# Second stage's input product by a seven-product block algorithm over pairs of token tiles, that stage ordered by the list scheduler

## The chip, the cores and the metric

One core of a Trainium2 chip runs the whole program in one launch. The metric is the device time of that launch in microseconds (us), the median of three runs. TensorE (PE) multiplies, VectorE (DVE), ScalarE (ACT) and GpSimd (POOL) work on vectors, and SyncE (SP) starts the DMA transfers. Each engine works off its own queue in program order and waits on semaphores for the others.

## The reference

Attention over 4 x 8 heads with 576 tokens (a banded mask for half of the heads, a dilated one for the others), whose output is the 2304 x 512 input of a gated layer, whose output is the input of a second layer:

```
def _moe2_ref(x, w_in, w_out, g_ln):          # 2304 tokens, 512 -> 1024 -> 512, float32
    h = x @ w_in
    h_max = np.max(h, axis=-1, keepdims=True)
    e = np.exp(h - h_max)
    sm = e / (np.sum(e, axis=-1, keepdims=True) + 1e-09)
    solu = h * sm
    mu = np.mean(solu, axis=-1, keepdims=True)
    var = np.mean((solu - mu) ** 2, axis=-1, keepdims=True)
    ln = (solu - mu) / np.sqrt(var + 1e-06) * g_ln
    return (ln @ w_out).astype(np.float32)
```

This second layer is the second stage; the change is about its first product, `h = x @ w_in`.

## The kernel before

**Products.** Every float32 operand is split into a high half (rounded to a short form) and a low half (the rest), and a product is three matmuls: high by high, high by low, low by high. One matmul takes 128 rows of the sum (k), 128 tokens and 512 columns. With the tokens' 128 x 128 block as the stationary operand, a tile of 128 tokens needs 2 column halves x 4 k blocks x 3 = 24 matmuls for `h` (`p_h`, L990 to L992) and 8 x 3 = 24 for the output (`p_products`, L1029 to L1031).

**First stage.** Attention and gated layer are ordered by a planner, the class `Plan`. A step has engines with estimated costs, needs, buffers that it takes and uses, and a due number. A simulated clock picks the steps one by one, and the order so found is the order of the instructions on every engine. The last steps of the first stage are the products `y` of the last 512 tokens; each of the four `y` banks is copied out (`yo`), stored to DRAM (`yT`), and read again by the second stage.

**Second stage.** It stands after the planned part, in an order written out by hand: `p_h(0)`, `p_h(1)`, then for each tile i `p_t(i)`, `p_h(i + 2)` and `p_o(i)`. After `p_h` come, for a 128 x 1024 tile, the maximum over the two banks of `h` (DVE L995), the exponential (ACT L997), three small operations and the product by `h` (DVE L1000), the square (ACT L1004), the subtraction of the mean (DVE L1005); then `p_t` turns the tile by 8 transposes on PE (L1015), with high halves by ACT (L1018) and low halves by DVE (L1019). `p_load` reads one tile of tokens back with one DMA (L974), and `p_split` makes its halves (L980, L981).

**Weights.** `prepare(2, ...)` turns the 16 blocks of `w_in` and `w_out` from 64 bit floats into split halves, in planned steps beside the last part of the first stage: per block a shift (ACT), `parts` and `joined` (DVE), `halves` (ACT), `lows` (POOL or DVE).

Of the kernel before, what the change touches and what calls it, by code (L numbers as in the profile page):

```python
# [240 lines left out]
def tile_attention_glu_solu(ctx: ExitStack, tc: tile.TileContext, qk_d, v_d, w1_d, win2_d, wout2_d,  # L241
# [14 lines left out]
    ps = pg.enter_context(tc.tile_pool(name="ps", bufs=1, space=PSUM, side="right"))
# [18 lines left out]
                 "yl": 3, "yh": 3, "pw": 2})  # L275
# [35 lines left out]
    def prepare(stage, f, cuts, srcs, scales, dues, needs=()):  # L311
# [658 lines left out]
    def p_load(i):  # L970
        y = pool["yp"].tile([P, KD, P], F32, tag="y", name="y", bufs=3)
        p = max(x for x in range(len(PARTS)) if start[x] <= i * P)
        a = i * P - start[p]
        nc.sync.dma_start(out=y, in_=yT[p][:, :, a:a + P])  # L974
        y2[i] = y

    def p_split(i):
        y = y2[i]
        yh = pool["yp"].tile([P, 2, KD, P], F32R, tag="yh", name="yh", bufs=3)
        nc.scalar.copy(yh[:, 0], y)  # L980
        nc.vector.tensor_tensor(yh[:, 1], y, yh[:, 0], ALU.subtract)  # L981
        y2[i] = yh

    def p_h(i):
        yh = y2.pop(i)
        h = pool["psh"].tile([P, 2, 512], F32, tag="h", name="h")
        for n in range(2):
            for k in range(KD):
                w = w2[divmod(2 * k + n, 3)]
                nc.tensor.matmul(h[:, n], yh[:, 0, k], w[:, 0], start=(k == 0), stop=False)  # L990
                nc.tensor.matmul(h[:, n], yh[:, 0, k], w[:, 1], start=False, stop=False)  # L991
                nc.tensor.matmul(h[:, n], yh[:, 1, k], w[:, 0], start=False, stop=(k == KD - 1))  # L992
        hf = h.rearrange("p a b -> p (a b)")
        st = pool["sp2"].tile([P, 8], F32, tag="st", name="st", bufs=3)
        nc.vector.tensor_reduce(st[:, 0:1], hf, AX.X, ALU.max, negate=True)  # L995
        e = pool["hp"].tile([P, FF2], F32, tag="e", name="e")
        nc.scalar.activation(e, hf, AF.Exp, bias=st[:, 0:1], accum_out=st[:, 1:2])  # L997
# [10 lines left out]
        ln_t[i] = (e, st)

    def p_t(i):  # L1010
        e, st = ln_t[i]
        tp = pool["pst"].tile([P, NF2, P], F32, tag="t", name="tp", bufs=1)
        lt = pool["hp"].tile([P, 2, NF2, P], F32R, tag="lt", name="lt")
        for k in range(NF2):
            nc.tensor.transpose(tp[:, k, :], e[:, k * P:(k + 1) * P], ident)  # L1015
        for q in range(2):
            c = slice(q * NF2 // 2, (q + 1) * NF2 // 2)
            nc.scalar.copy(lt[:, 0, c], tp[:, c])  # L1018
            nc.vector.tensor_tensor(lt[:, 1, c], tp[:, c], lt[:, 0, c], ALU.subtract)  # L1019
        ln_t[i] = (lt, st)  # L1020

    def p_products(i, ks, a=0, n=DM):
        lt, st = ln_t[i][0:2]
        if ks[0] == 0:
            ln_t[i] = (lt, st, pool["pst"].tile([P, n], F32, tag="o", name="o"))
        o = ln_t[i][2]
        for k in ks:
            w = w2[divmod(8 + k, 3)][:, :, a:a + n]
# [4 lines left out]

# [178 lines left out]
```

## Time and profile before

| | |
|---|---|
| device time, median of 3 runs | 758.14 us (757.66 to 759.91) |
| span of the profiled execution, first to last instruction | 756.9 us |
| PE busy | 744.9 us, 98% of the span |
| DVE, ACT, POOL busy | 399.8, 310.2, 105.3 us |
| second stage's first matmul | 538.02 us after the start |

A span is what the trace shows between the first and the last instruction. The profiled execution's own device time is not listed apart from it: the listed times lie 0.8 to 3.0 us above this span, the median 1.24 us. An engine is busy while an instruction runs on it; matmuls overlap in the pipeline, so the distance from start to start tells what one costs, not its duration.

### The profile page before, as it was taken

The page shows a single profiled execution, that of the slowest core. Times are in us where ns is not written, and L with a number is a line of the kernel's source. Part 1 is how long each engine was busy: PE and PEld are TensorE (multiplying, and loading weights), DVE is VectorE, ACT ScalarE, POOL GpSimd, SP SyncE. Part 2 cuts the span into 40 slices and gives each one's busy share as a digit, 9 for nine tenths or more (in the row PEclk, how much of TensorE's full clock was granted, in tenths as well). Part 3 has the DMA queues.
Part 4 walks back from the last instruction along what each step waited for, and adds up shares of the span by engine and source line. Part 5 has one row for each costly group of instructions (what it writes and reads, how often), then busy time and mean ns, then how long its engine had stood idle before and what let it go on. Part 6 is the DMA issues. An engine that isn't in the chain of part 4 may idle for free.

```text
span 756.9 us, 11671 instructions
## 1 busy us (share of the span) xinstructions
PE 744.9 (98%) x4691; PEld 622.8 (82%) x4691; DVE 399.8 (53%) x761; ACT 310.2 (41%) x718; POOL 105.3 (14%) x129
## 2 busy tenths in 40 slices
PE   8899999999999999999999999999999999999997
PEld 6788888899988887888888888888878888888886
DVE  3879996455444344444444437872354544445541
ACT  2876645355233243233334225541243343443433
POOL 0320322222300121201121200000020110101100
PEclk9999999999999999999999999999999999999999
DMA  9996103143021111041111045500201111111101
GB/s 330 405 402 260 33 4 114 64 149 110 16 87 39 61 49 51 0 155 53 71 70 51 1 153 202 187 1 1 69 20 38 56 45 40 55 29 57 49 22 42
DMA packets 34102, 68.90 MB, mean 91 GB/s; under 512 B 3200, under 2 KB 13440, under 8 KB 34048
## 3 DMA queue, kind: packets, MB, share of 16 engines
q1 hardware_dynamic: 34048, 68.16, 25.6%
q8 instruction: 37, 0.61, 0.3%
q14 instruction: 17, 0.14, 0.1%
HBM read 58.71 MB, written 9.44 MB: 90 GB/s over the span
## 4 chain that ended last, share of the span: by engine, by line
PE 93%; DMA 2%; DVE 2%; ACT 1%; SPq 1%; issue 0%; POOL 0%; ACTq 0%; DVEq 0%; POOLq 0%
PE y L850 7%; PE g L850 7%; PE vp L850 7%; PE g L851 7%; PE g L852 7%; PE y L852 7%; PE y L851 7%; PE vp L852 6%; PE vp L851 6%; PE o L1031 4%; PE h L992 4%; PE h L990 4%; PE h L991 4%; PE o L1029 4%; PE o L1030 4%; DMA raw<-w 2%
## 5 line engine op out<-in xcount | busy, mean ns | idle before, releaser
L850 PE MATMUL y<-uh,w 128*128 128x512 f32 (+1 forms) x244 | 91.6, 376 | 0.0
L852 PE MATMUL y<-uh,w 128*128 128x512 f32 (+1 forms) x244 | 89.2, 366 | 0.0
L851 PE MATMUL y<-uh,w 128*128 128x512 f32 (+1 forms) x244 | 89.1, 365 | 0.0
L881 ACT ACTIVATE u<-g 128x512 f32<-128x512 f32 (+1 forms) x61 | 33.5, 549 | 127.6 <-PE g L852 127.6
L887 DVE SCALAR_TENSOR_TENSOR u<-u,g 128x512 f32<-128x512 f32 (+1 forms) x61 | 38.1, 625 | 88.6 <-ACT u L881 88.4
L850 PE MATMUL vp<-xh,w 128*128 128x512 f32 (+1 forms) x196 | 77.9, 397 | 0.0
L850 PE MATMUL g<-xh,w 128*128 128x512 f32 (+1 forms) x196 | 77.6, 396 | 0.0
L852 PE MATMUL g<-xh,w 128*128 128x512 f32 (+1 forms) x196 | 76.1, 388 | 0.0
L851 PE MATMUL g<-xl,w 128*128 128x512 f32 (+1 forms) x196 | 76.0, 388 | 0.0
L852 PE MATMUL vp<-xh,w 128*128 128x512 f32 (+1 forms) x196 | 75.7, 386 | 0.0
L851 PE MATMUL vp<-xl,w 128*128 128x512 f32 (+1 forms) x196 | 75.5, 385 | 0.0
L891 DVE SCALAR_TENSOR_TENSOR u<-u,vp 128x512 f32<-128x512 f32 (+1 forms) x61 | 38.2, 626 | 53.2 <-PE vp L852 52.8
L286 ACT CAST uh<-u 128x512 fp32r<-128x512 f32 (+1 forms) x61 | 34.8, 571 | 75.0 <-DVE u L891 74.7
L1031 PE MATMUL o<-w,lt 128*128 128x512 f32 (+1 forms) x152 | 57.8, 380 | 0.2 <-DVE lt L1019 0.2
L1029 PE MATMUL o<-w,lt 128*128 128x512 f32 (+1 forms) x152 | 57.7, 380 | 0.0
L1030 PE MATMUL o<-w,lt 128*128 128x512 f32 (+1 forms) x152 | 57.5, 378 | 0.0
L990 PE MATMUL h<-w,yh 128*128 128x512 f32 x144 | 57.4, 399 | 0.0
L991 PE MATMUL h<-w,yh 128*128 128x512 f32 x144 | 56.1, 390 | 0.0
L992 PE MATMUL h<-w,yh 128*128 128x512 f32 x144 | 56.1, 390 | 0.0
L1006 POOL TENSOR_SCALAR st<-st 128x1 f32<-128x1 f32 x18 | 13.4, 745 | 287.3 <-ACT sq L1004 166.8
L850 PEld LDWEIGHTS y<-uh,w 128*128 128x128 f32 x244 | 46.0, 188 | 8.1
L852 PEld LDWEIGHTS y<-uh,w 128*128 128x128 f32 x244 | 46.0, 188 | 7.5
(127 smaller groups left out, 1490.5 us busy)
## 6 DMA issues: line engine op xcount, KB each, us to landing
raw<-w SPq DMA_DIRECT2D x36, 512.0 KB, 10.2
vt<-v SPq DMA_DIRECT2D x30, 256.0 KB, 2.7
qk<-qk SPq DMA_DIRECT2D x14, 400.0 KB, 3.7
y<-yT SPq DMA_DIRECT2D x18, 256.0 KB, 3.1
yT<-yo SPq DMA_DIRECT2D x16, 256.0 KB, 2.6
raw<-win SPq DMA_DIRECT2D x8, 512.0 KB, 5.8
raw<-wout SPq DMA_DIRECT2D x8, 512.0 KB, 4.1
out<-ob SPq DMA_DIRECT2D x16, 256.0 KB, 2.1
```

The lines of the kernel that those rows point to most:

```text
L286: nc.scalar.copy(dst, src) if scale is None else nc.scalar.mul(dst, src, scale)
L850: nc.tensor.matmul(acc, wh, xh, start=first, stop=False)
L851: nc.tensor.matmul(acc, wh, xl, start=False, stop=False)
L852: nc.tensor.matmul(acc, wl, xh, start=False, stop=last)
L887: return lambda e: nc.vector.scalar_tensor_tensor(out=u_of(f), in0=u_of(f), scalar=1.0, in1=T["g", v, f], op0=ALU.add, op1=ALU.mult)
L891: return lambda e: nc.vector.scalar_tensor_tensor(out=u_of(f), in0=u_of(f), scalar=0.5, in1=T["vp", v, f], op0=ALU.mult, op1=ALU.mult)
L990: nc.tensor.matmul(h[:, n], yh[:, 0, k], w[:, 0], start=(k == 0), stop=False)
L991: nc.tensor.matmul(h[:, n], yh[:, 0, k], w[:, 1], start=False, stop=False)
L992: nc.tensor.matmul(h[:, n], yh[:, 1, k], w[:, 0], start=False, stop=(k == KD - 1))
L1029: nc.tensor.matmul(o, lt[:, 0, k], w[:, 0], start=(k == 0), stop=False)
L1030: nc.tensor.matmul(o, lt[:, 0, k], w[:, 1], start=False, stop=False)
L1031: nc.tensor.matmul(o, lt[:, 1, k], w[:, 0], start=False, stop=(k == NF2 - 1))
```

## The change

The tokens are taken in nine pairs r of two tiles. A pair's input is a 2 x 2 block matrix of blocks of 128 tokens x 256 k (`a11`, `a12`, `a21`, `a22`), and `w_in` one of blocks of 256 k x 512 columns (`b11` to `b22`). The pair's `h` is then built from seven block products instead of eight, by Winograd's form of Strassen's algorithm:

- sums of the tokens (`p_sums`, four additions of 128 x 256): s1 = a21 + a22, s2 = s1 - a11, s3 = a11 - a21, s4 = a12 - s2
- sums of the weights, once: t1 = b12 - b11, t3 = b22 - b12, t2 = b22 - t1, t4 = b21 - t2
- p1 = a11 b11, p2 = a12 b21, p3 = s4 b22, p4 = a22 t4, p5 = s1 t1, p6 = s2 t2, p7 = s3 t3, each 2 k blocks x 3 = 6 matmuls into one PSUM bank
- p6 and p7 go on top of p1 in its bank `ha`, and p3 on top of p5 in `hb`; p2 is in `hc`, p4 in `hd`. Between them `ha` is copied out three times: s1 (= p1), u2 (= p1 + p6), u3 (= p1 + p6 + p7)
- four block sums, each with its maximum, in one DVE instruction: c11 = p1 + p2, c22 = u3 + p5, c21 = u3 + p4, c12 = u2 + p5 + p3

The exponential and what follows read `h` from SBUF now. The whole stage is planned steps; `line` fixes the order on PE, the planner that on the other engines. A pair is loaded with three DMAs into one of two buffers: pairs with even r into memory free since the attention ended, pairs with odd r into memory of the first stage, which opens at the step `switch`, after the last product of that stage. `w_in`'s blocks and sums are prepared by `operands`, seven blocks for each of the two k blocks.

```diff
-                 "yl": 3, "yh": 3, "pw": 2})
+                 "pw": 2, "ys0": 1, "ys1": 1, "yh0": 1, "yh1": 1,
+                 "hw0": 1, "hw1": 1, "ew0": 1, "ew1": 1, "lt": 2})
...
+        lead = (("in", 0), "joined", "b11")
+        due = 5000 + 30 * j
...
+        def split(x, needs):
+            plan.add((key, "halves", x), {"a": 0.63}, halves(x), needs + needs_of(home[x][0]), uses=[wf], due=due + 5)
+            plan.add((key, "lows", x), {"p": 1.27, "d": 0.68}, lows(x), [(key, "halves", x)], uses=[wf, st, (st, 1)], due=due + 5)
+
+        for x in ("b11", "b22", "b21"):
+            split(x, [(key, "joined", x)])
+        for x, a, b, free in (("t1", "b12", "b11", ["b11"]), ("t3", "b22", "b12", []), ("t2", "b22", "t1", ["b22"]),
+                              ("t4", "b21", "t2", ["b21"])):
+            before = {"t1": [(key, "joined", "b12")], "t3": [(key, "t1"), (key, "joined", "b22")], "t2": [(key, "t3")],
+                      "t4": [(key, "t2"), (key, "joined", "b21")]}[x]
+            plan.add((key, x), {"p": 1.27, "d": 0.68}, combined(x, a, b), before + [(key, "lows", y) for y in free],
+                     uses=[wf, st, (st, 1)], due=due + 6)
+            split(x, [(key, x)])
...
+    def p_load(r):
+        y = pool["y", r % 2].tile([P, 8, 2, P], F32, tag=f"y{r % 2}", name="y")
+        p = max(x for x in range(len(PARTS)) if start[x] <= r * TP)
+        a = r * TP - start[p]
+        nc.sync.dma_start(out=y[:, 1:3].rearrange("p c k t -> p (c k) t"), in_=yT[p][:, :, a:a + P])
+        for c in range(2):
+            nc.sync.dma_start(out=y[:, 3 * c], in_=yT[p][:, 2 * c:2 * c + 2, a + P:a + TP])
+        y2[r] = y
+
+    def p_sums(r, e):
+        y = y2[r]
+        for out_, a, b, op in ((4, 0, 3, ALU.add), (5, 4, 1, ALU.subtract), (6, 1, 0, ALU.subtract), (7, 2, 5, ALU.subtract)):
+            ENG[e].tensor_tensor(y[:, out_], y[:, a], y[:, b], op)
+
+    SETS = (slice(0, 3), slice(3, 7))
+
+    def p_high(r, h, e):
+        if r not in pairs:
+            pairs[r] = pool["y", r % 2].tile([P, 2, 7, 2, P], F32R, tag=f"yh{r % 2}", name="yh")
+        c = SETS[h]
+        put(e, pairs[r][:, 0, c], y2[r][:, 1 + c.start:1 + c.stop])
+
+    def p_low(r, h, e):
+        c = SETS[h]
+        less(e, pairs[r][:, 1, c], y2[r][:, 1 + c.start:1 + c.stop], pairs[r][:, 0, c])
...
+    def p_product(r, a, b, bank, more):
+        o, yh = p_bank(r, bank), pairs[r]
+        for j in range(2):
+            x = LEFT[a]
+            w = w_in[b, j]
+            first, last_ = j == 0 and not more, j == 1
+            nc.tensor.matmul(o, yh[:, 0, x, j], w[:, 0], start=first, stop=False, skip_group_check=True)
+            nc.tensor.matmul(o, yh[:, 0, x, j], w[:, 1], start=False, stop=False, skip_group_check=True)
+            nc.tensor.matmul(o, yh[:, 1, x, j], w[:, 0], start=False, stop=last_, skip_group_check=True)
+
+    def p_sum(r, row, col, kept, bank, n):
+        if n == 0:
+            rows_of[r, row] = pool["sp2"].tile([P, 10], F32, tag="st", name="st", bufs=8)
+        st = rows_of[r, row]
+        nc.vector.tensor_tensor_reduce(out=p_row(r, ("h", row))[:, col], in0=p_row(r, kept), in1=p_bank(r, bank), scale=1.0,
+                                       scalar=st[:, 8:9] if n else -3.4028234e38, op0=ALU.add, op1=ALU.max,
+                                       accum_out=st[:, 8 + n:9 + n])
...
+    def second_stage(stage_1, last):
...
+        add(("switch",), {"s": 0.0}, switch, stage_1, due=4000)
+
+        def pair_steps(r):
+            due = base + 22 * (r - 2)
+            ys, yh, hw, ew = ((x + str(r % 2), (x, r)) for x in ("ys", "yh", "hw", "ew"))
+            p = max(x for x in range(len(PARTS)) if start[x] <= r * TP)
+            add(("load", r), {"s": 1.6}, lambda e: p_load(r), [("opened",) if r % 2 == 0 else ("switch",)] +
+                [("store", p, k) for k in range(KD)], takes=[ys], due=due - 40)
+            add(("sums", r), {"p": 2.9, "d": 1.4}, lambda e: p_sums(r, e), [("load", r)], uses=[ys[1]], due=due - 20)
+            for h, (a, d) in enumerate(((0.85, 0.95), (1.1, 1.25))):
+                add(("yhigh", r, h), {"a": a}, lambda e, h=h: p_high(r, h, e), [("load", r)] + ([("sums", r), ("yhigh", r, 0)] if h else []),
+                    takes=[yh] if h == 0 else [], uses=[ys[1], yh[1]], due=due - 20)
+                add(("ylow", r, h), {"d": d}, lambda e, h=h: p_low(r, h, e), [("yhigh", r, h)], uses=[ys[1], yh[1]], due=due - 20)
+            banks = {x: ("h" + x, r) for x in "abcd"}
+            tags = dict(a="g", b="vp", c="a", d="a")
+
+            def product(x, a, b, bank, more, before):
+                add((x, r), {"t": 6 * mm}, lambda e: p_product(r, a, b, bank, more), before + [("ylow", r, int(a[0] == "s"))],
+                    takes=[] if more else [(tags[bank], banks[bank])], uses=[yh[1], banks[bank]], due=due)
+
+            def kept(x, after_, tile_, tags_):
+                add((x, r), {"a": 0.6, "d": 0.62}, lambda e: put(e, p_row(r, x), p_bank(r, "a")), [(after_, r)],
+                    takes=tags_, uses=[banks["a"], tile_[1]], due=due - 60)
+
+            def total(x, row, col, kept_, bank, n, before):
+                add((x, r), {"d": 0.75}, lambda e: p_sum(r, row, col, kept_, bank, n), before + [(kept_, r)],
+                    uses=[banks[bank], hw[1], ew[1]], due=due - 50)
+
+            product("p1", "a11", "b11", "a", False, [])
+            kept("s1", "p1", hw, [hw])
+            product("p5", "s1", "t1", "b", False, [])
+            product("p6", "s2", "t2", "a", True, [("s1", r)])
+            kept("u2", "p6", hw, [])
+            product("p2", "a12", "b21", "c", False, [])
+            total("c11", 0, 0, "s1", "c", 0, [("p2", r)])
+            product("p7", "s3", "t3", "a", True, [("u2", r)])
+            kept("u3", "p7", ew, [ew])
+            total("c22", 1, 1, "u3", "b", 0, [("p5", r)])
+            product("p4", "a22", "t4", "d", False, [])
+            total("c21", 1, 0, "u3", "d", 1, [("p4", r), ("c22", r)])
+            product("p3", "s4", "b22", "b", True, [("c22", r)])
+            total("c12", 0, 1, "u2", "b", 1, [("p3", r), ("c11", r)])
+            for row in (1, 0):
+                k = (r, row)
+                ends = [("c21", r)] if row else [("c12", r)]
+                add(("neg", *k), {"d": 0.16}, lambda e, row=row: p_neg(r, row), ends, due=due - 10)
+                add(("exp", *k), {"a": 1.3}, lambda e, row=row: p_exp(r, row), [("neg", *k)], uses=[hw[1], ew[1]], due=due)
+                add(("solu", *k), {"d": 1.85}, lambda e, row=row: p_solu(r, row), [("exp", *k)], uses=[hw[1], ew[1]], due=due)
+                add(("sqr", *k), {"a": 1.35}, lambda e, row=row: p_square(r, row), [("solu", *k), ("switch",)], uses=[ew[1]], due=due)
+                add(("centre", *k), {"d": 0.75}, lambda e, row=row: p_centre(r, row), [("sqr", *k)], uses=[ew[1]], due=due)
+                add(("var", *k), {"p": 1.3}, lambda e, row=row: p_spread(r, row), [("sqr", *k)], due=due)
...
+        line = [("out", last, NF1 - 1, 1)] + h(0, "p1", "p5", "p6", "p2", "p7", "p4") + h(1, "p1") + h(0, "p3") + \
+            h(1, "p2", "p5", "p6", "p7", "p4", "p3") + t(0)
+        for q in range(NP):
+            a, b, r = 2 * q, 2 * q + 1, q + 2
+            line += h(r, "p1", "p5", "p6") + [("o", a, 0, 0)] + t(b) + [("o", a, 0, 1)] + h(r, "p2", "p7", "p4")
+            if q < NP - 1:
+                line += [("o", b, 0, 0)] + h(r, "p3") + t(b + 1) + [("o", b, 0, 1)]
+        line += [("o", NT2 - 1, a, q) for a in (0, DM // 2) for q in range(2)]
+        for x, y in zip(line, line[1:]):
+            plan.steps[y]["needs"].append(x)
+            plan.steps[y]["after"].add(x)
 
```

**On PE, where the second stage begins.** Of before, the transposes of the first tile stand behind 48 matmuls of `h` (here the last two), and 24 more and the first output follow; one row of each group stands here.

```order
L991 MATMUL h_5251<-w2_1_4780,yh_4940 128x512
L992 MATMUL h_5251<-w2_1_4780,yh_4940 128x512
L1015 MATMUL tp_5291<-ident_83,e_5240 128x128 x8
L990 MATMUL h_5308<-w0_0_4626,yh_5005 128x512
...
L1029 MATMUL o_5346<-w2_2_4814,lt_5292 128x512
```

Of the change, the first row of each product is shown, six rows each: yh_4577 are the halves of pair 0, yh_5284 those of pair 1, so these are p1, p5, p6, p2, p7, p4 of pair 0, p1 of pair 1, p3 of pair 0, then p2, p5, p6, p7 of pair 1.

```order
L1110 MATMUL ha_5218<-win_4637,yh_4577 128x512
...
L1110 MATMUL hb_5231<-win_4666,yh_4577 128x512
...
L1110 MATMUL ha_5218<-win_4799,yh_4577 128x512
...
L1110 MATMUL hc_5251<-win_4679,yh_4577 128x512
...
L1110 MATMUL ha_5218<-win_4801,yh_4577 128x512
...
L1110 MATMUL hd_5272<-win_4810,yh_4577 128x512
...
L1110 MATMUL ha_5298<-win_4637,yh_5284 128x512
...
L1110 MATMUL hb_5231<-win_4720,yh_4577 128x512
...
L1110 MATMUL hc_5316<-win_4679,yh_5284 128x512
...
L1110 MATMUL hb_5332<-win_4666,yh_5284 128x512
...
L1110 MATMUL ha_5298<-win_4799,yh_5284 128x512
...
L1110 MATMUL ha_5298<-win_4801,yh_5284 128x512
```

Pair 1's first product, which reads halves of a pair loaded behind `switch`, has moved to the seventh place; behind it, p6 and p7 of pair 1 follow each other with nothing between them, and p3 of pair 1 stands one product behind p7.

**On DVE, at the same place.** Of before, the last two copies of `y`, then the first tile's chain:

```order
L290 COPY yo_5188<-y0_4559 128x512
L290 COPY yo_5194<-y2_4570 128x512
L995 TENSOR_REDUCE st_5238<-h_5213 128x1
L998 TENSOR_SCALAR st_5238<-st_5238 128x1
L999 RECIPROCAL st_5238<-st_5238 128x1
L1000 SCALAR_TENSOR_TENSOR e_5240,st_5238<-e_5240,st_5238,h_5213 128x1024
```

Of the change (the three `ISA` rows of 128x512 are c11, c22, c21 of pair 0; y_5260 is pair 1's input, and the row with x4 its four additions; yh_5284 128x768 are the low halves of its blocks a11, a12, a22):

```order
L290 COPY yo_5240<-y2_4568 128x512
L1118 ISA h_5238,st_5270<-h_5238,hc_5251 128x512
...
L1118 ISA h_5238,st_5281<-e_5279,hb_5231 128x512
...
L1118 ISA h_5238,st_5281<-e_5279,hd_5272,st_5281 128x512
...
L1124 TENSOR_SCALAR st_5281<-st_5281 128x1
L1064 TENSOR_TENSOR y_5260<-y_5260 128x256 x4
L295 TENSOR_TENSOR yh_5284<-y_5260,yh_5284 128x768
L1133 TENSOR_SCALAR st_5281<-st_5281 128x1
L1134 RECIPROCAL st_5281<-st_5281 128x1
L1135 SCALAR_TENSOR_TENSOR e_5279,st_5281<-e_5279,st_5281,h_5238 128x1024
```

Pair 1's additions and low halves stand behind c21 of pair 0, which reads `hd` and so the end of p4.

**On ACT, in a later pair.** lt are the high halves of the turned tiles, ha_5781 the bank of pair 4, e_5716 the rows of pair 3:

```order
L286 CAST lt_5771<-tp_5746 128x512
L286 CAST lt_5771<-tp_5753 128x512
L1128 ACTIVATE e_5716,st_5707<-h_5619,st_5707 128x1024
L1142 ACTIVATE sq_5779,st_5718<-e_5716,st_5718 128x1024
L286 CAST yh_5751<-y_5547 128x1024
L286 COPY h_5805<-ha_5781 128x512
```

The copy s1 (last row) stands behind two high halves, an exponential, a square and the high halves of a later pair. Before, ACT had no copy of `h` at all.

## Rows read from the trace of the kernel before

**Rows 1.** The page of the whole span: its head and part 1.

```profile
span 756.9 us, 11671 instructions
PE 744.9 (98%) x4691; PEld 622.8 (82%) x4691; DVE 399.8 (53%) x761; ACT 310.2 (41%) x718; POOL 105.3 (14%) x129
```

**Rows 2.** Waits of PE: engine, line, releaser: us in total, times, longest.

```profile
PE tp L1015 <- DVE e L1005: 1.1, 1, 1.1
```

**Rows 3.** Timeline of PE, start of the second stage: start, us, instruction [idle before].

```profile
538.02 0.39 PE L990 MATMUL h<-w,yh 128*128 128x512 f32 x1
...
543.24 0.39 PE L992 MATMUL h<-w,yh 128*128 128x512 f32 x1
...
548.67 0.39 PE L992 MATMUL h<-w,yh 128*128 128x512 f32 x1
550.14 1.09 PE L1015 MATMUL tp<-ident,e 128*128 128x128 f32 x8 [1.08 <-DVE e L1005]
```

**Rows 4.** The chain that ended last, in order of time: start, us, what.

```profile
543.66 1.24 DVE st L995
544.92 1.22 ACT e L997 x2
546.55 1.30 DVE e L1000 x2
...
549.34 0.76 DVE e L1005
...
562.42 0.87 PE tp L1015 x8
574.20 0.87 PE tp L1015 x8
```

**Rows 5.** Busy time by stretch: PE, PEld, DVE, ACT, POOL, PEclk, DMA, GB/s.

```profile
600.00:640.00 40.00, 40.00 (x191) 33.37 (x190) 19.29 (x33) 15.61 (x26) 3.87 (x6) 1.00 0.16 49
```

**Rows 6.** Groups of instructions by line and shape, DVE and ACT: busy, mean ns.

```profile
L1019 DVE TENSOR_TENSOR lt<-tp,lt 128x512 fp32r<-128x512 f32 x36 | 24.9, 691 | 20.0 <-ACT lt L1018 20.0
L295 DVE TENSOR_TENSOR uh<-u,uh 128x256 fp32r<-128x256 f32 x14 | 6.0, 427 | 3.1 <-ACT uh L286 3.0
L1000 DVE SCALAR_TENSOR_TENSOR e<-e,st,h 128x1024 f32<-128x1024 f32 x18 | 23.0, 1280 | 0.6
L1000 DVE DVE_READ_ACCUMULATOR e<-e,st,h 128x1 f32 x18 | 1.5, 82 | 0.0
...
L286 ACT COPY yo<-y 128x512 f32<-128x512 f32 x8 | 4.7, 586 | 14.5 <-PE y L852 12.3 <-DMA yT<-yo 2.3
...
L286 ACT CAST w<-wf 128x1536 fp32r<-128x1536 f32 x5 | 7.4, 1485 | 3.8 <-DVE wf L348 3.8
```

**Rows 7.** Timeline of SP, then ACT, at the stage's border; last, DMA issues: us to landing.

```profile
536.90 3.75 SPq L958 DMA_DIRECT2D yT<-yo  x4
540.71 0.53 SPq L974 DMA_DIRECT2D y<-yT  x1
...
539.72 0.59 ACT L286 COPY yo<-y 128x512 f32<-128x512 f32 x1 [2.27 <-DMA yT<-yo]
...
y<-yT SPq DMA_DIRECT2D x18, 256.0 KB, 3.1
```

**Rows 8.** Timelines of POOL and DVE late in the first stage.

```profile
426.41 2.55 POOL L295 TENSOR_TENSOR xl<-x,xh 128x512 fp32r<-128x512 f32 x2 [4.79 <-ACT xh L286]
...
428.08 1.43 DVE L295 TENSOR_TENSOR uh<-u,uh 128x512 fp32r<-128x512 f32 x1 [0.69 <-ACT uh L286]
```

**Rows 9.** Busy time by stretch, early in the program (columns of rows 5).

```profile
6.00:8.00 2.00, 0.26 (x2) 0.00 (x0) 0.00 (x0) 0.00 (x0) 0.00 (x0) 1.00 1.01 397
8.00:10.00 2.00, 1.70 (x32) 1.70 (x32) 0.00 (x0) 0.00 (x0) 0.00 (x0) 0.56 1.05 398
10.00:12.00 2.00, 2.00 (x23) 1.07 (x21) 1.38 (x2) 0.22 (x1) 0.00 (x0) 0.58 1.01 392
...
38.00:40.00 2.00, 0.47 (x5) 0.42 (x5) 1.90 (x5) 2.00 (x4) 0.00 (x0) 1.00 1.03 410
```

More of the change, by code (lines that the diff above doesn't have):

```diff
@@ L309, in tile_attention_glu_solu, with prepare @@
     w1, w2 = {}, {}
-    def prepare(stage, f, cuts, srcs, scales, dues, needs=()):
+    def prepare(stage, f, cuts, srcs, scales, dues, needs=(), lead=((1, 0), "joined", 0)):
         key = (stage, f)
@@ L368, in lows @@
             return emit
-        lead = (stage, 0)
         for i in range(m):
@@ L965, in tile_attention_glu_solu @@
     pool = {}
-    y2 = {}
-    ln_t = {}
+    y2, pairs, rows_of = {}, {}, {}
     start = [sum(size[:p]) for p in range(len(PARTS) + 1)]
[L970 to L997, printed above, removed]
+    NP = NT2 // 2
@@ new lines, in p_bank, with p_row @@
+    def p_bank(r, x):
+        if (r, x) not in keep:
+            tag, i = plan.where["h" + x, r]
+            keep[r, x] = (psy if tag[0] == "y" else ps).tile([P, 512], F32, tag=f"{tag}{i}", name=f"h{x}")
+        return keep[r, x]
+    def p_row(r, x):
+        if x in ("s1", "u2") or x[0] == "h":
+            if (r, "h") not in keep:
+                keep[r, "h"] = wp.tile([P, 6, 512], F32, tag=f"w{8 + r % 2}_0", name="h")
+            t = keep[r, "h"]
+        else:
+            if (r, "e") not in keep:
+                keep[r, "e"] = wp.tile([P, 6, 512], F32, tag=f"w{10 + r % 2}_0", name="e")
+            t = keep[r, "e"]
+        if type(x) is str:
+            return t[:, {"s1": 4, "u2": 5, "u3": 4}[x]]
+        return t[:, 2 * x[1]:2 * x[1] + 2]
@@ L1005, in p_h, with p_spread @@
         nc.vector.tensor_scalar(e, e, st[:, 4:5], None, ALU.add)
+    def p_spread(r, row):
+        st = rows_of[r, row]
         nc.gpsimd.tensor_scalar(st[:, 6:7], st[:, 5:6], 1.0 / FF2, 1e-6, ALU.mult, ALU.add)
         nc.gpsimd.tensor_tensor(st[:, 7:8], st[:, 6:7], mhalf[:, 0:1], ALU.pow)
[L1008 to L1020, printed above, removed]
@@ L1022, in p_products, with p_t @@
-    def p_products(i, ks, a=0, n=DM):
[L1023 to L1026, printed above, removed]
+    lt_of, o_of, tp_of = {}, {}, {}
+    HALF = NF2 // 2
+    def p_t(i, q):
+        e = flat(p_row(i // 2, ("e", i % 2)))
+        tag, n = plan.where["tp", i, q]
+        tp = tp_of[i, q] = psy.tile([P, HALF, P], F32, tag=f"{tag}{n}", name="tp")
+        for k in range(HALF):
+            c = (q * HALF + k) * P
+            nc.tensor.transpose(tp[:, k, :], e[:, c:c + P], ident)
@@ new lines, in p_lt @@
+    def p_lt(i, q, h, e):
+        if i not in lt_of:
+            lt_of[i] = pool["hp"].tile([P, 2, NF2, P], F32R, tag=f"lt{plan.where['lt', i][1]}", name="lt")
+        lt, tp, c = lt_of[i], tp_of[i, q], slice(q * HALF, (q + 1) * HALF)
+        if h == 0:
+            put(e, lt[:, 0, c], tp)
+        else:
+            less(e, lt[:, 1, c], tp, lt[:, 0, c])
+    def p_products(i, ks, a=0, n=DM):
+        lt = lt_of[i]
+        if (i, a) not in o_of:
+            tag, x = plan.where["o", i, a]
+            o_of[i, a] = psy.tile([P, 512], F32, tag=f"{tag}{x}", name="o")[:, 0:n]
+        o = o_of[i, a]
@@ L1027, in p_products @@
         for k in ks:
[L1028 removed]
+            w = w2[5 + k // 3, k % 3][:, :, a:a + n]
             nc.tensor.matmul(o, lt[:, 0, k], w[:, 0], start=(k == 0), stop=False)
```

180 lines of the change are left out of this document (126 added, 54 removed).

## The prediction

> **What bounds the kernel now.** I read the head of the page first: PE is busy for 744.9 of 756.9 us [rows 1]. A busy PE need not be at its limit, so the next question is whether it waits. In the list of PE's waits only one entry of over 0.3 us lies in the second stage, 1.1 us [rows 2]. The timeline shows where [rows 3]: the stage's 48 first matmuls start from 538.02 to 548.67, 47 steps of 0.2266 us without a gap, and then the first transposes wait until 550.14 for the subtraction of the mean. From there the stage runs in even steps: transposes at 562.42 and at 574.20, 11.78 us for a tile [rows 4], which is 48 matmuls x 0.2266 + 0.87 of transposes with 0.03 left. Beside it DVE is busy for 19.3 of 40 us and ACT for 15.6 [rows 5]. So the stage is bound by the number of matmuls that PE is given, and a matmul less is worth 0.2266 us as long as no other engine makes PE wait. The question is where it will.
>
> **What the change removes.** A pair of tiles takes 7 x 6 = 42 matmuls for `h` in place of 48: 6 x 0.2266 = 1.36 us a pair, 9 pairs: **-12.2 us**. The order confirms the number (54 matmuls fewer). Transposes and output products stay, 2 x 0.87 and 48 matmuls a pair, so a pair should take 90 x 0.2266 + 1.74 = 22.1 us where it took 23.56. The old wait ahead of the first transposes goes with its place, and about 0.2 us of a small wait in the last tiles: **-1.3**.
>
> **What it adds beside PE.** For 128x512 DVE needs 0.69 us and for 128x256 0.43 [rows 6], so 0.26 for 256 columns more: 0.96 for 768, 1.22 for 1024. ACT needs 0.59 and, for 1536, 1.49 [rows 6]: 0.81 for 768, 1.04 for 1024. The block sum with maximum (`ISA`) does not occur before. It is bounded below by 0.69, what one pass over 512 columns costs, and above by 1.36, the 1024 column product with its accumulator [rows 4, 6]; it is a pass over 512 with an accumulator, so I take 0.77. A pair then costs DVE: additions 4 x 0.43, low halves 0.96 + 1.22, block sums 4 x 0.77, one of the copies 0.69, small operations 1.3, products by `h` 2 x 1.36, means 2 x 0.75, low halves of the turned tiles 4 x 0.69, a copy out 0.69: 16.6 us of 22.1. ACT: 0.81 + 1.04, two copies 1.2, exponentials and squares 4 x 1.25, 4 x 0.59, 0.67: 11.1. Neither is the bound, but both run closer to it, and with an order that is fixed beforehand.
>
> The preparation of the weights gains six blocks' halves and eight sums, partly on POOL, while the last part of the first stage runs. The order on PE is the same there. DVE's chain from one product to the next has some 3 us to spare (the u of one round is used after 24 matmuls, 5.4 us, and takes some 2.3), so I count nothing. Without that cover it costs what the chain is late by.
>
> **The start of the stage.** Here a new wait appears. Pair 1 is loaded behind `switch`; its DMA stands on SP behind the four stores of `y`, which end at 540.7 now [rows 7]. ACT's last copy of `y`, at 539.72 [rows 7], now stands behind copy s1 of pair 0, which can start at 538.02 + 5 x 0.2266 + 0.42 (from the last matmul's start at 543.24 to DVE's at 543.66 [rows 3, 4]) = 539.6 and ends at 540.2: 0.5 later. So the loads go out from 541.2 and, at 3.1 us and three issues, land by 545.2. That is early enough; the order on DVE is not. There the additions for pair 1 stand behind c21 of pair 0, and that reads p4, PE's sixth product: last start 538.02 + 35 x 0.2266 = 545.95, so c21 runs from 546.4 to 547.2, the negation to 547.4, the additions to 549.1 and the low halves to 550.0. PE wants them for the third matmul of p1 of pair 1, at 538.02 + 38 x 0.2266 = 546.6, and every product behind it waits too. PE loses **3.4 us**. ACT is not the last here: u3 of pair 0 ends at 545.6, the high halves of pair 1 at 546.5.
>
> I follow the queues on in the same way. p5 of pair 1 waits 0.1 for c12 of pair 0 (553.7). p6 and p7 stand together, and between them ACT must copy u2: 0.42 + 0.59 after the last start of p6, against 0.23: **0.8 us**. p3 stands one product (1.36) behind p7, and needs u3 and c22: 0.42 + 0.69 + 0.82 - 0.23 = 1.7: **0.4**. The transposes of the first tile want the mean's subtraction, which waits for c21 of pair 1 on DVE: **0.2**. Together 3.4 + 0.1 + 0.8 + 0.4 + 0.2 = **+4.9 us**; PE's first output product then starts with everything ready.
>
> **The clock behind that wait.** PE would be without work for some 3 us, from 546.9 to 550.0. Early in the program it worked for only 0.26 us from 6 to 8, and the granted clock then was 0.56 and 0.58 for the next two stretches of 2 us, the lower of the two levels (1.2 GHz) for about 3.4 us of the 4; in the stretch from 38 to 40, with 1.53 us without work, it stayed at 1.00 [rows 9]. The new gap is longer than either. A fall like the first costs half of 3.4 us, 1.7; part of it lies in a stretch where PE waits anyway: **+1.4**. The Trainium skill ("TensorE: Matmul & The Clock Gate", section "What's actually happening") says that the throttled clock is the default state and activity releases it. By that rule the gap lowers the clock; by the row at 38 to 40 alone it need not. The sum is 1.4 us less without it.
>
> **In the even part** I looked for a step of PE with little cover. p6 needs copy s1, and p5 covers it: 1.36 + 0.23 - 0.42 - 0.59 leaves 0.5. On ACT that copy stands behind two high halves, an exponential, a square and 1024 columns of high halves, a row of 5.2 us that begins 0.2 after the transposes, and PE has 2.72 + 1.36 + 1.36 = 5.4 us of work from the transposes to p6. So p6 comes out between 0 and some 0.5 us late, in five pairs: 0 to 2.5, I take **+0.4**, since such rows overlap by up to 0.1 each. All other steps have a product or an output half between them.
>
> POOL does the additions for some pairs. In the trace a DVE subtraction with both inputs in SBUF took 1.43 us instead of 0.69 beside two POOL subtractions [rows 8]. The Trainium skill ("SBUF — State Buffer", the rules on the shared port pair) says that such a DVE instruction and a POOL one that reads SBUF exclude each other. The trace agrees. At up to 0.74 for four operations a pair that is 3 us, DVE at 19.6 of 22.1, still not the bound.
>
> **The sum.** Against the profiled span: 756.9 - 12.2 - 1.3 + 4.9 + 1.4 + 0.4 = 750.1. The median of the listed runs is 1.24 above that span, so **751.3 us**.
>
> **The rivals.**
> - *The clock holds.* All as above without the 1.4: 749.9. For it speaks the row at 38 to 40; against it the length of the gap.
> - *Queues in the even part.* ACT or DVE makes PE wait in every pair, by copy s1 or by a block sum that takes 1.36. 0.4 us more in each of 9 pairs give 754.9. Speaks for it: 5.2 against 5.4 us; against: DVE 16.6 of 22.1.
> - *No change that can be measured* (a measurement here tells 0.3%, 2.3 us). The same waits at 0.6 to 1.1 us a pair, or the weights late in the first stage: 756 to 760.
> - *DVE becomes the bound, and the kernel slower.* Its place is the whole stage. From 23.2 us of DVE a pair on (9 x (23.2 - 23.56) + 4.9 + 1.4 - 1.3 = +1.8, so some 760) the time is above before's; that needs 6.6 us more than my sum, where block sums at 1.36 (+2.4) and POOL's interference (+3.0) make 5.4. Two upper bounds at once are not enough.
> - *The wait at the start is smaller*, because the transfers or the `ISA` are quicker than my rows: down to 4.0 for the five terms, and no fall of the clock: 749.
>
> **How the numbers follow.** Chances: forecast 0.42, clock holds 0.27, small start 0.06, queues in the even part 0.13, no change 0.08, slower 0.04. The first four are faster by over 0.3%: 0.87 (0.01 off for a case that I don't see), the next 0.08, the last 0.05. The likeliest case's own range is 750 to 753. The range from 748.5 to 754.8 takes in the small start (749) and 0.4 us of waits in every pair, and leaves out the last two cases and a part of the one ahead of them.
>
> **What would show it.** In the changed profile: 42 matmuls of `h` a pair at 0.227; PE idle for about 3.4 us just behind p4 of pair 0, released by DVE's low halves; an `ISA` of about 0.7; PEclk under 1 in the stretch behind the gap; transposes of every second tile 22.1 to 22.5 us apart. It would be wrong if the 22.1 came out over 23.2, if the last part of the first stage ended later than 538, or if PE waited in that stage for a block of weights.

## The result, and the profile after

The changed kernel took 750.96 us (median of 4 runs, 749.95 to 751.75) beside 758.34 us for the kernel before: a ratio of 0.9897, 95% interval 0.988 to 0.9914. It is faster by about 1%; 751.3 was forecast.

The page of the changed kernel, its head and part 1 (to read against [rows 1]):

```profile
span 748.2 us, 11769 instructions
PE 734.1 (98%) x4637; PEld 613.0 (82%) x4637; DVE 439.3 (59%) x868; ACT 322.4 (43%) x734; POOL 130.7 (17%) x156
```

PE has 54 matmuls fewer, DVE 39.5 us more to do. All waits of PE from 530 us to the end, of the changed kernel (engine, line, releaser: us in total, times, longest):

```profile
PE ha L1112 <- DVE st L1133: 2.4, 1, 2.4
PE ha L1110 <- ACT h L286: 0.7, 1, 0.7
PE ha L1110 <- ACT yh L286: 0.3, 1, 0.3
PE hb L1110 <- DVE st L1118: 0.2, 1, 0.2
```

Where [rows 2] had one wait of over 0.3 us, four stand here. PE's timeline shows where they are:

```profile
537.31 0.39 PE L1110 MATMUL ha<-win,yh 128*128 128x512 f32 x1
...
545.25 0.39 PE L1112 MATMUL hd<-win,yh 128*128 128x512 f32 x1
545.97 0.50 PE L1110 MATMUL ha<-win,yh 128*128 128x512 f32 x1 [0.33 <-ACT yh L286]
546.30 0.40 PE L1111 MATMUL ha<-win,yh 128*128 128x512 f32 x1
549.14 0.65 PE L1112 MATMUL ha<-win,yh 128*128 128x512 f32 x1 [2.45 <-DVE st L1133]
549.59 0.63 PE L1110 MATMUL ha<-win,yh 128*128 128x512 f32 x1
...
553.12 0.40 PE L1110 MATMUL hc<-win,yh 128*128 128x512 f32 x1
...
557.00 0.39 PE L1112 MATMUL ha<-win,yh 128*128 128x512 f32 x1
558.06 0.50 PE L1110 MATMUL ha<-win,yh 128*128 128x512 f32 x1 [0.68 <-ACT h L286]
558.40 0.39 PE L1111 MATMUL ha<-win,yh 128*128 128x512 f32 x1
...
561.23 0.50 PE L1110 MATMUL hb<-win,yh 128*128 128x512 f32 x1 [0.15 <-DVE st L1118]
...
562.80 1.09 PE L1163 MATMUL tp<-ident,e 128*128 128x128 f32 x8
```

The first is p1 of pair 1, whose first matmul waits for the high halves and whose third for the low ones. The releaser is printed as the small operation at 549.01; DVE's timeline shows what PE waited for, the row ahead of it:

```profile
545.77 0.75 DVE L1118 CUSTOM_DVE_ANT_0 h<-e,hd,st 128x512 f32<-128x512 f32 x1
546.44 0.08 DVE L1118 DVE_READ_ACCUMULATOR2_ANT st<- 128x1 f32 x1
546.56 0.15 DVE L1124 TENSOR_SCALAR st<-st 128x1 f32<-128x1 f32 x1
546.67 1.55 DVE L1064 TENSOR_TENSOR y<-y 128x256 f32<-128x256 f32 x4
548.14 0.95 DVE L295 TENSOR_TENSOR yh<-y,yh 128x768 fp32r<-128x768 f32 x1
549.01 0.15 DVE L1133 TENSOR_SCALAR st<-st 128x1 f32<-128x1 f32 x1
```

The block sum c21 of pair 0, the additions and the low halves of pair 1 follow each other without a gap. Behind the wait matmuls start some 0.43 apart instead of 0.2266. The busy time by stretch (PE, PEld, DVE, ACT, POOL, PEclk, DMA, GB/s):

```profile
546.00:548.00 2.00, 0.70 (x2) 0.26 (x2) 1.93 (x7) 1.24 (x2) 0.00 (x0) 1.00 0.00 0
548.00:550.00 2.00, 0.85 (x2) 0.68 (x3) 1.93 (x5) 1.04 (x1) 0.00 (x0) 0.83 0.02 4
550.00:552.00 2.00, 2.00 (x6) 1.60 (x5) 1.96 (x4) 0.89 (x2) 0.00 (x0) 0.50 0.00 0
552.00:554.00 2.00, 2.00 (x8) 1.59 (x8) 0.68 (x2) 1.51 (x3) 0.75 (x2) 0.81 0.26 73
...
564.00:600.00 36.00, 36.00 (x172) 30.05 (x171) 26.64 (x56) 20.10 (x34) 11.09 (x16) 1.00 0.21 66
```

PE all but stops from 546.7 to 549.1, and the granted clock is at the lower of the two levels (1.2 GHz) from some time after 549 to before 554. In the even part PE has no wait. The chain that ended last has the transposes of every second tile 22.2 us apart:

```profile
582.52 0.87 PE tp L1163 x8
...
604.73 0.87 PE tp L1163 x8
```

### The profile page after: what moved, and what is told of

Read it like the earlier page. It is cut to its first block, busy times and chain, and to the rows that moved or that the text cites. A ratio compares the mean times of both kernels' runs of the same rounds, so it can differ in the third digit from the quotient of the medians.

```text
span 748.2 us, 11769 instructions
## 1 busy us (share of the span) xinstructions
PE 734.1 (98%) x4637; PEld 613.0 (82%) x4637; DVE 439.3 (59%) x868; ACT 322.4 (43%) x734; POOL 130.7 (17%) x156
## 4 chain that ended last, share of the span: by engine, by line
PE 94%; DMA 3%; DVE 1%; ACT 1%; SPq 0%; issue 0%; DVEq 0%
PE y L849 7%; PE g L849 7%; PE vp L849 7%; PE g L850 7%; PE g L851 7%; PE y L851 7%; PE y L850 7%; PE vp L851 7%; PE vp L850 7%; PE o L1183 4%; PE o L1184 4%; PE o L1182 4%; PE pv L631 2%; PE tp L1163 2%; PE sp L585 2%; PE ha L1112 2%
## 5 line engine op out<-in xcount | busy, mean ns | idle before, releaser
L731 POOL TENSOR_TENSOR sq<-x 128x256 f32<-128x256 f32 x28 | 18.6, 666 | 211.6 <-DVE x L290 179.5
L295 DVE TENSOR_TENSOR uh<-u,uh 128x512 fp32r<-128x512 f32 (+1 forms) x61 | 43.8, 717 | 15.1 <-ACT uh L286 14.5
L849 PEld LDWEIGHTS y<-uh,w 128*128 128x128 f32 x244 | 46.0, 188 | 8.1
L851 PEld LDWEIGHTS y<-uh,w 128*128 128x128 f32 x244 | 46.0, 188 | 7.5
L850 PEld LDWEIGHTS y<-uh,w 128*128 128x128 f32 x244 | 46.1, 189 | 7.0
L598 ACT ACTIVATE s<-s,nm 128x64 f32<-128x64 f32 x120 | 40.2, 338 | 22.7 <-DVE nm L593 22.7
## 6 DMA issues: line engine op xcount, KB each, us to landing
raw<-w SPq DMA_DIRECT2D x36, 512.0 KB, 10.2
```

What stands on the lines that cost most here:

```text
L295: ENG[e].tensor_tensor(dst, a, b, ALU.subtract)
L598: nc.scalar.activation(T[s_][:, i], T[s_][:, i], AF.Exp, bias=st["nm"][:, i:i + 1], accum_out=sm[:, i:i + 1])
L849: nc.tensor.matmul(acc, wh, xh, start=first, stop=False)
L850: nc.tensor.matmul(acc, wh, xl, start=False, stop=False)
L851: nc.tensor.matmul(acc, wl, xh, start=False, stop=last)
```

## The experiments

Each ran beside the kernel before on its own chip: again, early, order and fill on one (where the kernel before took 759.41), chain, twice, less7 and sums2 on a second (759.26), chain_2 and fine on a third (758.58). What is compared with again from another chip carries that difference of 0.15 (0.83 on the third). Medians carry a spread of about 1 us that has nothing to do with the second stage: its first matmul starts between 537.26 and 541.09 in the twelve profiles, with the same order on PE ahead of it. So I also give the **stage**, from that start to the end of the span. It is 218.88 before (756.9 - 538.02) and 210.89 after (748.2 - 537.31).

| run | median, us | ratio, interval | stage, us | first matmul to first transposes |
|---|---|---|---|---|
| again | 751.37 | 0.9893 (0.9875 to 0.9912) | 210.9 | 25.5 |
| early | 754.23 | 0.9931 (0.9912 to 0.9951) | 213.8 | 21.1 |
| order | 750.69 | 0.9886 (0.9867 to 0.9906) | 210.6 | 23.3 |
| fill | 749.12 | 0.9865 (0.9845 to 0.9886) | 209.3 | 23.9 |
| chain | 746.26 | 0.9828 (0.9808 to 0.9847) | 206.4 | 21.1 |
| twice | 763.52 | 1.0055 (1.0034 to 1.0075) | 222.8 | 27.9 |
| less7 | 739.54 | 0.9732 (0.971 to 0.9754) | 197.7 | 21.9 |
| sums2 | 761.53 | 1.0027 (1.0015 to 1.004) | 220.6 | 29.0 |
| chain_2 | 746.51 | 0.9839 (0.9824 to 0.9855) | 206.4 | 21.0 |
| fine | 745.91 | 0.9832 (0.9817 to 0.9847) | 204.7 | (another order) |

**again.** No edit.

> The changed kernel, unedited, on the chip on which the next three run. Its listed runs were 749.95 to 751.75, two near 750.1 and two near 751.7. Expected: 750 to 752, ratio to the kernel before 0.988 to 0.9915. In its first profile the second stage began at 537.31 us where it began at 538.02 before, though the order on PE in the first stage is the same; if that 0.7 us is only a spread from run to run, the stage should begin elsewhere between 537 and 539 in this profile, with the same 25.5 us from its first matmul to its first transposes.

The stage began at 538.80 and took the same 210.9 us. That it began 0.7 earlier in the first profile was spread. The medians fell by 7.4 and 8.0 us where the stage shrank by 8.0: they show no change of the first stage.

**fill.** What did the fall of the clock cost, and did the gap bring it?

```diff
+            if (r, a, j) == (1, "a11", 0):
+                idle = psy.tile([P, 512], F32, tag=plan.where["o", 0, 0][0] + str(plan.where["o", 0, 0][1]), name="idle")
+                for _ in range(11):
+                    nc.tensor.matmul(idle, pairs[0][:, 0, 0, 0], w[:, 0], start=True, stop=True)
             nc.tensor.matmul(o, yh[:, 1, x, j], w[:, 0], start=False, stop=last_, skip_group_check=True)
```

> Eleven more matmuls of 512 columns, into a bank that nobody reads, stand ahead of the third matmul of p1 of pair 1, where PE waits: 11 x 0.2266 = 2.5 us of work in the 2.45 us gap. The waits stay as they are. Theory (the gap lowers the clock): the granted clock stays at 1.00 from 548 to 554 and the 1.7 us come back, 749.3. Rival (the clock falls for another reason, or its fall costs nothing since PE waits anyway): no change, 751.

Windows of the run fill at the same place (columns as above):

```profile
548.00:550.00 2.00, 2.00 (x10) 1.66 (x9) 1.97 (x5) 1.73 (x3) 0.00 (x0) 1.00 0.01 4
550.00:552.00 2.00, 2.00 (x10) 1.46 (x10) 1.90 (x7) 0.94 (x2) 0.00 (x0) 1.00 0.00 0
```

With work that nobody uses in the gap, the clock stays at 1.00, the stage is 1.6 us shorter than that of again, and the median is 749.12 where 749.3 was expected. The other waits, 0.42, 0.68 and 0.15 us, are those of again (0.40, 0.68 and 0.15). So the gap brings the fall, and the fall costs 1.6.

**early** and **order.** Two ways to take the low halves of pair 1 from behind c21: load the pair earlier, or change the order alone.

```diff
-        y = pool["y", r % 2].tile([P, 8, 2, P], F32, tag=f"y{r % 2}", name="y")
+        b = 0 if r == 1 else r % 2
+        y = pool["y", b].tile([P, 8, 2, P], F32, tag=f"y{b}", name="y")
...
-            add(("load", r), {"s": 1.6}, lambda e: p_load(r), [("opened",) if r % 2 == 0 else ("switch",)] +
+            add(("load", r), {"s": 1.6}, lambda e: p_load(r), [("opened",) if r % 2 == 0 or r == 1 else ("switch",)] +
...
```

> Pair 1 is loaded into the buffer of pair 0 as soon as pair 0's halves are made, ahead of switch, so that its additions, high halves and low halves don't stand behind c21 of pair 0. Theory (the wait at the start is the late low halves of pair 1, 0.33 + 2.45 us, and it brings the fall of the clock, 1.7 us): both go, the span from the stage's first matmul to its first transposes shrinks from 25.5 to about 21 us, the time by 4.5, to some 746.5; what is left are the 0.7 of p7 of pair 1 behind copy u2 and 0.15 of p3. Rival (the wait only moves on, to p5 of pair 1 behind c12 of pair 0 or to the first transposes behind the mean): about half comes, 748.7. Rival (the clock falls for another reason): 748.2, with a granted clock under 1 still in the stretches from 548 to 554.

```diff
-            add(("sums", r), {"p": 2.9, "d": 1.4}, lambda e: p_sums(r, e), [("load", r)], uses=[ys[1]], due=due - 20)
+            add(("sums", r), {"p": 2.9} if r == 1 else {"p": 2.9, "d": 1.4}, lambda e: p_sums(r, e), [("load", r)], uses=[ys[1]], due=due - 20)
...
-        for x, y in zip(line, line[1:]):
+        for x, y in list(zip(line, line[1:])) + [(("ylow", 1, 0), ("c21", 0)), (("ylow", 1, 1), ("solu", 0, 1))]:
```

> The load of pair 1 stays behind switch; only the order changes: the low halves of pair 1's first three blocks stand ahead of c21 of pair 0 on DVE, its additions on POOL, the other low halves ahead of the product by h of pair 0. Theory (the transfer is early enough, the order on DVE is late): transfer lands at 545.1 as before, high halves 0.83, low halves 0.95, so PE waits to about 547.0 instead of 549.1, some 0.9 in all, and a gap that short leaves the clock at 1.00: 2.0 + 1.7 = 3.6 less, 747.3. Rival (the load behind switch and the four stores is what is late): the wait stays at over 2 us and the time within 1 us of the changed kernel's.

Both were wrong in the time. PE's waits from 530 us on, first of early, then of order:

```profile
PE hb L1113 <- DVE yh L295: 3.0, 1, 3.0
PE ha L1113 <- DVE yh L295: 2.1, 1, 2.1
PE ha L1111 <- DVE h L290: 0.8, 1, 0.8
PE hb L1111 <- DVE st L1119: 0.6, 1, 0.6
```

```profile
PE hb L1112 <- DVE yh L295: 1.6, 2, 1.3
PE ha L1110 <- ACT h L286: 1.6, 1, 1.6
PE ha L1110 <- ACT yh L286: 0.6, 1, 0.6
PE ha L1112 <- DVE yh L295: 0.3, 1, 0.3
```

In both the long wait at p1 of pair 1 went as the theory has it (none in early, 0.56 + 0.26 in order, with the clock at 1.00 to 564). In order the load still stands behind `switch`, so the order on DVE was what was late there; the transfer, with the high halves behind it, accounts for the 0.56 at most. But in early, 21.1 us to the first transposes were followed by p1 and p5 of pair 2, which waited 2.13 and 3.02 us for their low halves, and a fall of the clock there (0.95 from 564 to 600). In order, p7 of pair 1 waited 1.57 us for copy u2, which the planner had put on ACT behind a square that waited for DVE, and p5 of pair 2 waited 1.27. One wait gone, the list scheduler's next one appeared: a place that none of my theories had named.

**chain.** The loads as in early, with the buffers shared so that pair 2 comes first behind `switch`, and the order around the first transposes written out:

```diff
...
+        y = pool["y", (r + (r > 0)) % 2].tile([P, 8, 2, P], F32, tag=f"y{(r + (r > 0)) % 2}", name="y")
...
+        low = [("sums", 2), ("c12", 0), ("solu", 0, 1), ("ylow", 2, 0), ("u2", 1), ("c11", 1), ("solu", 0, 0), ("c22", 1),
+               ("centre", 0, 1), ("c21", 1), ("centre", 0, 0), ("c12", 1), ("ylow", 2, 1), ("lt", 0, 0, 1)]
+        for x, y in list(zip(line, line[1:])) + list(zip(low, low[1:])) + [(("exp", 1, 1), ("s1", 2)), (("s1", 2), ("exp", 1, 0)), (("s1", 2), ("yhigh", 3, 0))]:
...
```

> As in the run early, pair 1 is loaded ahead of switch; the two buffers are now shared so that pair 2 is the first to be loaded behind it, and the order on DVE around the first transposes is fixed: low halves of pair 2 ahead of the copy u2 of pair 1 and of the low halves of the first turned tile, and on ACT copy s1 of pair 2 ahead of the high halves of pair 3. Theory (early lost what it won because the low halves of pair 2 then stood behind late work on DVE, 2.13 + 3.02 us and a fall of the clock): 21.1 us from the stage's first matmul to its first transposes as in early, against 25.5, no wait of over 1 us behind them, and 4.4 us less than the changed kernel run on the same chip (751.4): 747.0. Rival (the waits move on once more, to pair 3 or to copy s1): 749 to 752.

All of PE's waits in the stage, of chain:

```profile
PE ha L1110 <- DVE h L290: 0.9, 1, 0.9
PE tp L1163 <- DVE e L1147: 0.3, 1, 0.3
```

746.26 (747.0 expected), and 4.5 us off the stage. This bears out the account of the start: the forecast had added 4.8 for the wait for the low halves and the clock's fall together. The run changes loads, buffers and order at once, so it does not price each of them.

**chain_2** and **fine.** Is the rest, p7 behind copy u2, there because p6 and p7 stand together?

```diff
-            h(1, "p2", "p5", "p6", "p7", "p4", "p3") + t(0)
+            h(1, "p6", "p2", "p7", "p5", "p4", "p3") + h(2, "p1") + t(0)
...
-            line += h(r, "p1", "p5", "p6") + ...
+            line += h(r, *(["p1"] if q else []), "p5", "p6") + ...
...
```

> The kernel of the run chain once more, as the base of the run fine on the same chip: 745.5 to 747.5, ratio to the kernel before 0.981 to 0.985.

> On top of the loads of chain, the order on PE is changed so that no product stands directly behind one whose copy or sum it needs: for pair 1 p6, p2, p7, p5, p4, p3, and p1 of pair 2 ahead of the first transposes; DVE and ACT are ordered to suit. Theory (the wait of p7 of pair 1 for copy u2 is there because p6 and p7 stand together): the 0.93 of that wait and the 0.34 of the first transposes in chain go, 1.2 less than chain, 745.0, ratio about 0.981. Rival (DVE, busy for 1.93 to 2.0 of every 2 us there in chain, is the bound of that stretch, and the wait only moves to the first transposes or to p5 of pair 2): within 0.5 of chain.

In fine no wait of PE is left in the stage; it is 1.6 us shorter than in chain_2 (1.2 expected). DVE, at 1.7 to 2.0 of every 2 us, was just enough. The medians differ by 0.6 with overlapping intervals, and the rival had said within 0.5: the times don't decide. The waits and the stage, one profile of fine against two of chain's kernel that agree to 0.1, speak for the theory. Both beat the changed kernel and the one before.

**twice.** The price of a product.

```diff
-        for j in range(2):
+        for j in (0, 1) * (2 if a == "a22" else 1):
```

> p4 is computed twice in every pair, into the same bank, the second time over the first: eight block products a pair, as many matmuls as before the change, everything else as in the changed kernel. Theory (the stage is bound by PE's matmuls): 9 x 6 x 0.2266 = 12.2 us more than the changed kernel, 763.6, and 23.5 us between the transposes of every second tile where it is 22.2. That is some 4 us above the kernel before: what the new start costs. Rival (other engines set the pace in part, so that a matmul more is hidden): under 10 us more.

12.15 us more than again, 12.2 expected; the stage is 11.9 longer. The chain of twice has the transposes of every second tile 23.56 us apart, as [rows 4] have it:

```profile
590.11 0.87 PE tp L1163 x8
...
613.67 0.87 PE tp L1163 x8
```

**less7.** The same from the other side.

```diff
-        for j in range(2):
+        for j in range(0 if a == "s3" else 2):
```

> p7 is left out in every pair (the lower row of h and the copy u3 are then without s3 t3): six block products, all other work as in the changed kernel. Theory (PE bound, and DVE and ACT have room below 22.2 us a pair): 12.2 less, and 0.7 more of the wait of p7 of pair 1: 738.4, with 20.8 us between the transposes of every second tile. Rival (DVE or ACT sets the pace soon under 22 us, as the sum of 16.6 us for DVE with waits between would have it): 740 to 746.

```profile
588.48 0.87 PE tp L1163 x8
...
609.32 0.87 PE tp L1163 x8
```

20.84 us a pair with no wait behind the start: DVE and ACT keep up with six products. The median, 739.54, lies between the theory's 738.4 and the rival's 740 to 746; the distance of the transposes decides for the theory. The stage is 13.2 us shorter; the waits at the start came in other pieces (1.70, 1.19 and 1.61) that left the clock at 1.00.

**sums2.** How much room has DVE?

```diff
+        for _ in range(2):
+            nc.vector.tensor_tensor_reduce(out=p_row(r, ("h", row))[:, col], in0=p_row(r, kept), in1=p_bank(r, bank), scale=1.0,
...
```

> Every block sum with its maximum is computed twice on DVE: 4 x 0.77 = 3.1 us more of DVE a pair, 19.5 of 22.2, and more than what 1.36 us for one would have added (2.4). Theory (in the even part DVE has that much room): no new wait of PE between 580 and 735; the start is later by the sums c22 and c21 of pair 0 that stand ahead of the low halves of pair 1, 2 x 0.77 = 1.5, and by about 1 more in pair 1: 754. Rival (the queues close in every pair): at 0.4 to 1 us in each of 8 pairs 757 to 762.

Here my theory fell and the rival held. PE's waits from 580 to 735 us, and ACT's timeline ahead of one of them:

```profile
PE ha L1110 <- ACT h L286: 4.2, 5, 1.1
```

```profile
613.30 1.15 ACT L1129 ACTIVATE e<-h,st 128x1024 f32<-128x1024 f32 x1 [1.71 <-DVE st L1125]
614.36 0.18 ACT L1129 ACTIVATION_READ_ACCUMULATOR e<-h,st 128x1 f32 x1
614.45 1.14 ACT L1143 ACTIVATE sq<-e,st 128x1024 f32<-128x1024 f32 x1
615.49 0.18 ACT L1143 ACTIVATION_READ_ACCUMULATOR sq<-e,st 128x1 f32 x1
615.58 1.03 ACT L286 CAST yh<-y 128x1024 fp32r<-128x1024 f32 x1
616.51 0.58 ACT L286 COPY h<-ha 128x512 f32<-128x512 f32 x1
```

The exponential waits 1.71 us for a maximum that DVE has ready later, and copy s1, on which p6 waits (1.07 us at 617.14), stands behind it, a square and 1024 columns of high halves. DVE had 2.8 us more to do a pair (464.0 us busy for 439.1 in again; 3.1 forecast), and the kernel was 10.2 us slower than again, its stage 9.7. Of these, 3.5 lie ahead of the first transposes (2.5 forecast) and some 6 behind them, although from 597.96 to 691.72 DVE was busy for only 16.7 to 18.7 us of each pair's 23.4 to 23.6.

## Why the prediction was right, step by step

**The bound.** "A matmul less is worth 0.2266 us as long as no other engine makes PE wait": shown by twice (+12.15 for 54 matmuls) and by less7, with 23.56, 22.2 and 20.84 us a pair.

**The start.** From start to start, less 0.2266 for each matmul between, the rows of after give 3.2 us for p1 of pair 1 (545.25 to 549.14, three steps; forecast 3.4), 0.95 for p7 (557.00 to 558.40, two steps; 0.8) and 0.4 for p3 (0.4, though the forecast's own numbers, 1.70 less 1.36, give 0.34); the 0.1 and 0.2 forecast for p5 and the first transposes were not there. 4.6 in all, for 4.9. The cause was put right: c21 of pair 0 ran from 545.77, which is 8.46 after the stage's first matmul (8.4 forecast), and the low halves came behind it. Order shows it by the wait at p1 that it takes away.

**The clock.** The ten matmul steps from 549.14 to 553.12 took 3.98 us in place of 2.27: 1.7 us, for 1.4. The part that the forecast had put into PE's waiting was not there: 0.83 from 548 to 550 is 0.7 us at the lower level, and PE works again from 549.14. Fill shows that the gap is its cause, at 1.6. The rival that the clock holds is out. The rule that the forecast weighed (the Trainium skill, "TensorE: Matmul & The Clock Gate", section "What's actually happening": the throttled clock is the default, and activity releases it) agrees with this trace at 0.50 from 550 to 552, behind the gap.

**The even part.** The term of +0.4 was mis-sized: nothing was lost. ACT's timeline in one pair, then PE's, whose first transposes there start at 604.56:

```profile
605.50 1.07 ACT L286 CAST lt<-tp 128x512 fp32r<-128x512 f32 x2
...
609.73 0.59 ACT L286 COPY h<-ha 128x512 f32<-128x512 f32 x1
...
610.89 0.39 PE L1110 MATMUL ha<-win,yh 128*128 128x512 f32 x1
```

Copy s1 ended at 610.32 and p6 started at 610.89, unwaited: over 0.5 us were left. The row on ACT was shorter than the 5.2 us of the forecast: 4.3 us to the end of the high halves at 609.77, 4.8 with the copy. Sums2 shows that the place was the right one, and that the rival of queues in every pair is a real one: what it lacked here was a later maximum.

**The old waits.** -1.3 was too small. PE's timeline of the kernel before, near its end:

```profile
739.62 0.39 PE L1031 MATMUL o<-w,lt 128*128 128x512 f32 x1
...
740.93 0.50 PE L1031 MATMUL o<-w,lt 128*128 128x512 f32 x1 [0.18 <-DVE lt L1019]
```

These three steps of matmuls lost 0.6 where I had counted 0.2, and the first wait is 1.24 from start to start (548.67 to 550.14 [rows 3]). So about -1.9.

**The sum.** The stage shrank by 8.0 where the terms gave 6.8: 0.4 and 0.6 are the two steps above, the start and the clock (0.3 too much, 0.3 too little) cancel, and some 0.2 stays unassigned. That the median came within 0.4 us is partly luck: the stage was 1.2 us shorter than forecast, but the runs lie 1.75 us above their spans (749.95 over 748.2), where I had taken 1.24, and the median is 1.0 above the profiled run.

**DVE.** 26.64 of 36 us are 16.4 a pair, for 16.6. But in that stretch pairs are prepared faster than they are used (additions start at 569.57, 581.95 and 597.32); from 604.73 to 693.52 DVE is busy for 13.9 to 14.7 of every 22.2 us. The block sum took 0.69, or 0.75 where it continues a maximum, and the 0.08 of its accumulator lie inside that (0.77 forecast, between 0.69 and 1.36). But the point from which the rival "DVE becomes the bound" should decide, 23.2 us a pair by adding up, was put wrong: sums2 was already slower than the kernel before (761.53 for 759.26) with DVE busy for 16.7 to 18.7 us of a pair. With queues in a fixed order, lateness counts long before the sum does. The interference of POOL that I had bounded at 3.0 us a pair was small: POOL did the additions of only three pairs (from 556.83, 569.57 and 581.95), and beside them a product by `h` at 557.40 took 1.37 instead of 1.28 and the subtraction of the mean at 569.82 took 1.05 instead of 0.75 us. By the Trainium skill ("SBUF — State Buffer", section "Who interferes with whom") the pair of ports that DVE and POOL share is an exclusive lock, which could give such rows; no run here isolates it.

## What to carry to other kernels

A saving on the engine that is the bound is worth its instructions times their distance, and can be counted beforehand; what it gives back is found by following each in-order queue at the place where the pipeline starts, one late row after the other. Where such a wait is taken away, look at once for the row that is late next: two of three repairs here moved it, and of those tried only an order written out for DVE and ACT as well, up to the first even tile, kept the gain. An engine's free time is no measure of its room: 2.8 us more a pair, in a chain that another queue stands behind, lengthened the stage by 9.7 us, although DVE was still free for 4.8 us or more of each pair from 597.96 to 691.72.

## What the runs showed of the hardware that was not expected

- A wait costs more than its entry in the list: the step behind one was 0.33 to 0.34 us in place of 0.23 (545.97 to 546.30, 558.06 to 558.40).
- Waits of 1.70 and 1.19 us with two matmuls between left the clock at 1.00 (less7), as did 1.57 in order; 2.45 behind 0.33 brought it to 0.50. The fall does not stand at a fixed place behind the gap: in sums2 it shows before PE works again (0.91 from 550 to 552, work from 551.94), in twice only after (1.00 from 552 to 554, 0.90 from 554 to 556, work from 554.19).
- The stage's first matmul started between 537.26 and 541.09 us with one order on PE. The granted clock of the first 40 us lay at 0.91, 0.96 or 1.00, but that alone does not explain it: 1.00 stands beside 539.77 (fine) and 537.77 (less7). The two latest starts, of twice (541.09) and fine, go with 0.97 from 40 to 100 us, where the other ten profiles have 1.00, and PE's waits for the first stage's loads (`qkv`) sum to anything from 1.7 to 4.2 us. What share each has stays open.
- DVE's product by `h`, with its inputs in SBUF, took 1.73 us beside POOL's additions in early (550.69) and 1.28 without them (555.79). Not every row beside POOL grew: low halves beside its additions in order took 0.96 (547.34), and 0.95 without them in the changed kernel (548.14).
